# A spectral gate on one core: a rewritten order list, with cosine and sine parts of ten even and five odd row slots split between ScalarE and VectorE

## The chip, the cores and the metric

The kernel runs on one core of one Trainium2 chip. The metric is device time in microseconds for one execution. Before the change the median of three runs is 117.61 us (117.53 to 118.46).

A core has five instruction streams that run side by side and wait for one another through semaphores. TensorE (PE) multiplies matrices into PSUM. VectorE (DVE) and ScalarE (ACT) copy, cast and combine; both read PSUM. GpSimd (POOL) does element-wise work on SBUF. SyncE (SP) issues almost all DMAs here. Each stream executes its instructions in the order in which they stand, so an instruction that waits holds back everything behind it on its own engine.

## The reference

```python
def _A_ref(x, w_r, w_i):
    X = rfft2(x.astype(float32), axes=(-2, -1))
    X = X * (w_r + 1j * w_i)
    return irfft2(X, s=(S, D), axes=(-2, -1)).astype(bfloat16)
...
x = A_x
g = sigmoid((x * gate_w).sum(-1, keepdims=True))
return g * _A_ref(x, A_w_r, A_w_i) + (1 - g) * _B_ref(x, B_w_r, B_w_i)
```

x is 2048 x 1024 in bfloat16. Both filters act on the same x, so the forward transform is made once, multiplied by two sets of weights, and the two inverse transforms are mixed with the gate g, one number for each row.

## The kernel before, in words

All transforms are matrix multiplications. The 2048 rows are 16 groups s1 of 128; the 1024 columns are folded four ways, so that the even and the odd column frequencies (parity 0 and 1) are two separate problems of half the size.

The program is written out by hand. A string `ORDER` holds some 590 tokens, and a loop at the end calls one small function for each token. Nothing is rescheduled: the order of the tokens is the order on each engine's stream and on SP's DMA stream. A token names the step, its indices, the PSUM banks (0 to 7) that it uses, and for copies the engine (A for ScalarE, D for VectorE, P for GpSimd). The steps, with the lines that the profile shows for them:

- `x`, `c`, `W`: loads of x, of constants and of the 16 weight tiles (L252 to L264, L276), all on SP but for two small ones, the constant F1 and the gate column gws, which ScalarE issues. Each of the eight DMA slots of a queue is reused by the eighth DMA after it, which waits for it. `tab` (L298, L299) makes ScalarE load its function table.
- First stage. `F1:s1:e/o` (L334) multiplies row group s1 for one parity into half a bank for each of two halves; the two halves have to be added and subtracted into `y`. Either `FC` copies one half to a scratch tile (L204 on ScalarE, L206 on VectorE) and `FD` folds on VectorE (L382, two instructions), or `FX` copies both and `FP` folds on GpSimd (L382 on POOL, two instructions). The scratch tiles are eight slots in `wx`, used in turn (`tmp`). `gc` prepares gate coefficients on GpSimd and needs gws.
- Middle stage, for n = 0 to 15 (0 to 7 even, 8 to 15 odd). `F2` (L450) and its copies `T`, `F3` (L480) and its copy `X`, `P` (L494, VectorE: two products of 128x2048 elements with the weights), `J` (L537), whose result two copies `R` bring to SBUF tiles `rl` (five in use at once), and two `H` (L549) that store them, 256 KB each, to a scratch area in DRAM. `NA` and `N` patch one column. `GH` to `GW` make the gate and multiply it into the matrices EA and EB.
- The turn through DRAM. `L:par:v` (L554) reads 512 KB of the scratch back in another layout; each needs all H of its parity.
- Last stage, for eight row slots v and two s. `V:par:v:s` (L565) and its copy `VC`, then `U` (L581) or `C` (L590). `U` gives the row transform for both halves of the columns; `C`, half the matmul columns, gives its cosine and sine parts, whose sum and difference are the two halves. For the even parity the result is kept in `EV`: `EX` copies both parts to scratch and `EQ` (L615) adds and subtracts them, or `E` copies. For the odd parity `OR` (L635, VectorE) adds or subtracts EV and the PSUM bank into the output tile, `OC` and `OP` (L631) do so through a copy and GpSimd, `QD` and `QP` (L642, L647) for parts. `S` (L652) stores the slot.

What orders the stages: `y` of all groups of one parity before its `F2`; H of a parity before its L; L:0 before `V:0`; L:1 before `V:1`.

Of the kernel before, what the change touches and what calls it, by code (L numbers as in the profile page):

```python
# [24 lines left out]
warm:8 c:A:F1 c:A:gws tab:A x:S:0:1 x:S:1:1 x:S:2:2 x:S:4:2 x:S:6:2 x:S:8:2 x:S:10:2 x:S:12:2 x:S:14:2 c:S:FD:0:1  # L25
F1:1:o:0 F1:1:e:1 FX:1:o:D F1:0:o:2 FC:1:e:D F1:0:e:3 FP:1:o FD:1:e F1:3:o:0 F1:2:e:4 FC:0:e:D F1:3:e:1 gc:P FD:0:e
F1:2:o:5 FC:3:e:A FC:2:e:D F1:4:e:3 FD:3:e FX:2:o:A F1:5:o:6 FX:0:o:A FD:2:e F1:5:e:5 FC:4:e:A FP:0:o FX:3:o:A FD:4:e
F1:6:e:1 FC:5:e:A F1:4:o:2 FD:5:e FC:6:e:A F1:7:e:0 FP:2:o c:S:WF:0:4 FD:6:e F1:6:o:3 W:S:0 FC:7:e:A F1:9:e:7 FD:7:e
FX:6:o:A F1:8:e:1 FP:3:o FC:9:e:D c:S:WJ:0:4 F1:11:e:3 FD:9:e F1:10:e:0 c:S:w0 FC:11:e:A F1:7:o:4 c:S:PM FC:8:e:A
FP:6:o FD:11:e FX:5:o:A c:S:EZ F1:13:e:5 FC:10:e:A FD:8:e W:S:1 F1:12:e:6 FP:5:o FD:10:e c:S:WF:4:16 FC:12:e:A  # L30
F1:14:e:1 FC:13:e:A FD:12:e FX:4:o:A F1:15:e:3 W:S:2 F1:15:o:0 FD:13:e FP:4:o FC:15:e:A F1:11:o:2 FC:14:e:A FD:15:e
FC:15:o:A F1:8:o:6 c:S:WJ:4:16 F1:14:o:5 FD:14:e FC:8:o:A F1:10:o:3 neg:A:0:4 FD:15:o FC:14:o:A F1:12:o:7 FX:7:o:A
# [680 lines left out]
```

## Time and profile before

| | us |
|---|---|
| median of three runs | 117.61 |
| span of the profiled execution | 115.6 |
| PE busy in the span | 103.6 |
| VectorE busy | 97.0 |
| ScalarE busy | 84.4 |
| GpSimd busy | 46.2 |
| first F1 matmul | 4.87 |
| first product (P) starts | 24.53 |
| first even read-back (L:0:0) issued | 62.28 |
| first odd read-back issued | 83.95 |
| first odd V matmul | 89.17 |

Groups of the page that the change touches (line, engine, operation, out<-in, count; busy and mean ns of one; idle time before them and what ended it):

```profile
L615 POOL TENSOR_TENSOR re<-wx 128x256 f32<-128x256 f32 x28 | 19.6, 730 | 55.3 <-DMA re<-sc 53.1
L204 ACT CAST rl<-ps 128x1024 bf16<-128x1024 f32 x29 | 29.6, 1142 | 0.7 <-ACT wx L204 0.7
L494 DVE TENSOR_TENSOR p<-X,ro 128x2048 bf16<-128x2048 bf16 x16 | 19.1, 1215 | 0.0
L382 DVE TENSOR_TENSOR y<-ps,wx 128x256 bf16<-128x256 f32 x48 | 16.4, 412 | 0.1
L635 DVE TENSOR_TENSOR ot<-re,ps 128x512 bf16<-128x512 f32 x22 | 13.8, 681 | 0.4
```

Two instructions that follow each other on an engine overlap a little, so in a run of equal ones the distance from start to start is less than the mean time of one. The distance is what counts when work is summed.

### The profile page before, as it was taken

The numbers are of one execution on the slowest core, as the hardware profiler recorded it, in microseconds if no ns is written. First come the engines' busy times: TensorE is split into PE (matmuls) and PEld (weight loads), VectorE is DVE, ScalarE is ACT, GpSimd is POOL, SyncE is SP. The second block draws the span as 40 slices with busy tenths as digits, with TensorE's granted clock in tenths as the row PEclk, the third lists the DMA queues.
The fourth block names the chain that finished last, engine by engine and source line by source line (L and its number), as shares of the span: only waits on it lengthen the run. The fifth ranks groups of instructions, "written<-read, shape, count | busy, mean of one in ns | idle before, by whom it ended". The sixth has DMA issues, their size and how long they took to land.

```text
span 115.6 us, 3953 instructions
## 1 busy us (share of the span) xinstructions
PE 103.6 (90%) x1619; PEld 71.3 (62%) x1619; DVE 97.0 (84%) x164; ACT 84.4 (73%) x138; POOL 46.2 (40%) x74
## 2 busy tenths in 40 slices
PE   5999999999999699898889899989979999999900
PEld 2499989875567256463445357459859765867400
DVE  0099999999999999999899999999157349999970
ACT  4009488999999999999999999977735844534300
POOL 1066995900000000000000000057986999999920
PEclk9999999999999999999999999999999999999995
DMA  3999999999579999669999999999999992482874
GB/s 90 348 326 401 403 374 367 363 397 408 210 222 324 371 394 373 169 263 397 350 293 354 348 306 401 254 357 382 352 353 411 403 418 98 198 346 119 327 279 181
DMA packets 17794, 36.79 MB, mean 318 GB/s; under 512 B 1904, under 2 KB 10736, under 8 KB 17776
## 3 DMA queue, kind: packets, MB, share of 16 engines
q1 hardware_dynamic: 17488, 36.44, 87.5%
q8 instruction: 12, 0.20, 0.6%
q10 hardware_dynamic: 288, 0.10, 0.4%
q14 instruction: 6, 0.05, 0.1%
HBM read 23.96 MB, written 12.58 MB: 316 GB/s over the span
## 4 chain that ended last, share of the span: by engine, by line
PE 39%; DVE 19%; DMA 16%; ACT 16%; issue 4%; SPq 1%; DVEq 1%; ACTq 0%
ACT rl L204 11%; PE ps L581 9%; PE ps L565 8%; DVE y L382 7%; PE ps L450 6%; PE ps L334 5%; DMA sc<-rl 5%; DMA re<-sc 4%; DMA ig<-cst_ig 4%; PE ps L537 3%; DMA re<-in_x_dram 3%; PE ps L480 3%; DVE p L494 3%; ACT X L204 3%; PE ps L590 3%
## 5 line engine op out<-in xcount | busy, mean ns | idle before, releaser
L615 POOL TENSOR_TENSOR re<-wx 128x256 f32<-128x256 f32 x28 | 19.6, 730 | 55.3 <-DMA re<-sc 53.1
L204 ACT CAST rl<-ps 128x1024 bf16<-128x1024 f32 x29 | 29.6, 1142 | 0.7 <-ACT wx L204 0.7
L204 ACT COPY wx<-ps 128x256 f32<-128x256 f32 (+1 forms) x39 | 17.2, 498 | 10.5 <-PE ps L334 8.2
L537 PE MATMUL ps<-p,wj 32*64 32x512 bf16 x512 | 20.5, 381 | 2.5 <-ACT rl L204 2.0
L204 ACT CAST V<-ps 128x512 bf16<-128x512 f32 x25 | 13.8, 601 | 11.3 <-PE ps L565 8.4
L494 DVE TENSOR_TENSOR p<-X,ro 128x2048 bf16<-128x2048 bf16 x16 | 19.1, 1215 | 0.0
L450 PE MATMUL ps<-fd,y 128*128 128x256 bf16 x128 | 16.5, 273 | 0.4 <-ACT rl L204 0.4
L382 DVE TENSOR_TENSOR y<-ps,wx 128x256 bf16<-128x256 f32 x48 | 16.4, 412 | 0.1
L334 PEld LDWEIGHTS <-re 128*128 128x128 bf16 x256 | 15.2, 100 | 1.6 <-DMA re<-in_x_dram 1.0
L334 PE MATMUL ps<-f,re 128*128 128x128 bf16 x256 | 15.8, 224 | 0.3
L204 ACT CAST T<-ps 128x512 bf16<-128x512 f32 x26 | 15.5, 693 | 0.0
L537 PEld LDWEIGHTS <-wj 32*64 32x64 bf16 x512 | 8.4, 103 | 10.6 <-issue 7.5
L382 POOL TENSOR_TENSOR y<-wx 128x256 bf16<-128x256 f32 x16 | 11.1, 734 | 8.2 <-DVE wx L206 5.9
L635 DVE TENSOR_TENSOR ot<-re,ps 128x512 bf16<-128x512 f32 x22 | 13.8, 681 | 0.4
L450 PEld LDWEIGHTS <-y 128*128 128x128 bf16 x128 | 11.5, 97 | 4.1 <-issue 2.6
L581 PE MATMUL ps<-ig,V 128*128 128x512 bf16 x56 | 13.4, 380 | 0.0
L204 ACT CAST X<-ps 128x1024 bf16<-128x1024 f32 x12 | 13.2, 1118 | 0.0
L206 DVE COPY wx<-ps 128x512 f32<-128x512 f32 (+1 forms) x10 | 5.8, 578 | 7.4 <-PE ps L334 4.8
L480 PE MATMUL ps<-T,wf 64*64 64x256 bf16 (+1 forms) x128 | 10.2, 332 | 1.1 <-DVE np L514 1.0
L590 PE MATMUL ps<-ig,V 128*128 128x256 bf16 x72 | 9.7, 273 | 0.0
L494 DVE TENSOR_TENSOR p<-X,wx 128x2048 bf16<-128x2048 bf16 x8 | 9.4, 1217 | 0.0
L494 DVE TENSOR_TENSOR p<-X,y 128x2048 bf16<-128x2048 bf16 x8 | 9.3, 1215 | 0.0
(60 smaller groups left out, 138.4 us busy)
## 6 DMA issues: line engine op xcount, KB each, us to landing
sc<-rl SPq DMA_DIRECT2D x32, 256.0 KB, 4.7
ro<-in_we_dram SPq DMA_DIRECT2D x8, 512.0 KB, 8.3
re<-sc SPq DMA_DIRECT2D x8, 512.0 KB, 6.1
ro<-sc SPq DMA_DIRECT2D x8, 512.0 KB, 7.7
re<-in_x_dram SPq DMA_DIRECT2D x7, 512.0 KB, 8.0
out_dram<-ot SPq DMA_DIRECT2D x7, 512.0 KB, 2.6
wx<-in_wo_dram SPq DMA_DIRECT2D x4, 512.0 KB, 6.6
y<-in_wo_dram SPq DMA_DIRECT2D x4, 512.0 KB, 5.0
```

Source lines behind the costliest of these rows:

```text
L204: nc.scalar.copy(out=out, in_=in_)
L334: nc.tensor.matmul(o, lhsT=lh, rhs=rh, start=(h == 0), stop=(h == 1))
L382: Q[e].tensor_tensor(yo[:, v, k:k + n, s1, :], a.rearrange("p (k c) -> p k c", c=4), b.rearrange("p (k c) -> p k c", c=4), op)
L450: nc.tensor.matmul(ps[:, v * 256:v * 256 + 256], lhsT=y[:, v, par, b, 2 * t:2 * t + 2, :, :].rearrange("p j s c -> p (j s c)"), rhs=C["FD" ...
L480: nc.tensor.matmul(view(ps[ho, tt * 512:(tt + 1) * 512], dst), lhsT=lh, rhs=view(T[hp(jh), tt, :], src), start=(w == 0), stop=(w == 1))
L494: nc.vector.tensor_tensor(p[:, r], xb, w, ALU.mult)
L537: nc.tensor.matmul(o, lhsT=lh, rhs=src[r, ri, wi, tt], start=(q == 0), stop=(q == 3))
L565: nc.tensor.matmul(ps[:, ch * 128:ch * 128 + 128], lhsT=RR[par][:, v, ch // 2, s, c0 + 256 * ab:c0 + 256 * ab + 128], rhs=Ew[:, s1, :], st ...
L581: nc.tensor.matmul(ps, lhsT=Vs[par, v][:, s, ch, :], rhs=rh, start=(ch == 0), stop=(ch == 3))
L590: nc.tensor.matmul(ps[:, o:o + 256], lhsT=Vs[par, v][:, s, ch, :], rhs=g[:, o:o + 256], start=(ch % 2 == 0), stop=(ch % 2 == 1))
L615: Q[e].tensor_tensor(EV[:, v, s, 256 * h:256 * h + 256], t[:, 0], t[:, 1], (ALU.add, ALU.subtract)[h])
L635: nc.vector.tensor_tensor(otile(v)[:, s, h, :], EV[:, v, s], PS["O", 1, v, s], (ALU.add, ALU.subtract)[h])
```

## The change

`ORDER` is replaced as a whole; three functions change and two are new. The arithmetic of the result is the same.

```diff
 ORDER = """
-warm:8 c:A:F1 c:A:gws tab:A x:S:0:1 x:S:1:1 x:S:2:2 x:S:4:2 x:S:6:2 x:S:8:2 x:S:10:2 x:S:12:2 x:S:14:2 c:S:FD:0:1
...
-F3:13:6 R:10:0:A P:12:0 X:13:A H:10:0 J:11:0:4 L:0:4 P:12:1 R:10:1:A F3:14:6 R:11:0:A X:14:D F2:15:0:2 F2:15:1:3
-T:15:0:A P:13:0 T:15:1:A J:12:0:6 R:11:1:A V:0:0:1:2 P:13:1 R:12:0:A F3:15:4 V:0:0:0:3 R:12:1:D X:15:A H:12:0
-V:0:1:0:0 H:10:1 V:0:1:1:1 L:0:5 VC:0:1:0:A P:14:0 H:11:0 J:13:4:6 VC:0:0:0:A VC:0:1:1:A P:14:1 VC:0:0:1:A R:13:0:A
-P:15:0 J:14:0:2 R:13:1:A H:13:0 H:11:1 C:0:0:1:4 P:15:1 H:12:1 C:0:0:0:5 EX:0:0:D R:14:0:D R:14:1:A EX:0:1:A H:14:1
-J:15:6:2 H:13:1 EQ:0:1:0:P V:0:2:0:4 EQ:0:0:0:P C:0:1:1:5 R:15:0:D R:15:1:A H:14:0 C:0:1:0:0 EQ:0:0:1:P H:15:1
-V:0:2:1:1 VC:0:2:0:A GW:D:8 V:0:3:1:2 H:15:0 EX:1:1:A L:0:6 V:0:3:0:3 VC:0:2:1:A EX:1:0:D L:0:7 EQ:1:1:0:P C:0:2:0:4
-VC:0:3:0:D VC:0:3:1:A C:0:2:1:1 EQ:1:0:0:P V:0:4:1:0 EX:2:1:D EQ:0:1:1:P V:0:4:0:5 C:0:3:0:2 EQ:2:1:0:P VC:0:4:0:A
...
-L:1:7 C:0:6:1:2 EQ:2:1:1:P EX:6:1:A EQ:5:1:0:P VC:0:7:0:A VC:0:7:1:D E:3:1:D C:0:7:1:3 V:1:0:0:1 V:1:0:1:4 EQ:4:1:0:P
...
-S:S:3 OR:6:1:0 S:S:6
...
+warm:8 tab:A c:A:F1 x:S:0:1 F1:0:e:7 F1:0:o:1 x:S:8:2 c:S:WF:0:4 F1:9:e:5 F1:8:e:2 FC:0:e:D FC:0:o:A FD:0:e x:S:1:1 FD:0:o
+c:A:gws x:S:14:2 F1:8:o:6 F1:9:o:3 F1:1:e:1 F1:1:o:7 neg:P:0:4 FC:9:e:A gc:P FX:8:e:A FD:9:e F1:14:o:0 x:S:10:2 FC:8:o:D
+FX:1:e:A FC:1:o:A F1:15:o:2 FP:8:e F1:14:e:5 x:S:2:2 F1:15:e:1 FC:9:o:D x:S:4:2 FD:8:o FC:14:o:A F1:10:o:6 FD:9:o FX:15:o:A
...
+F1:3:o:6 FD:6:e FD:6:o FC:5:o:A FC:3:o:A F1:12:o:0 F2:1:0:5 FX:12:o:A FD:5:o F2:1:1:1 c:S:EZ T:1:0:A F2:0:1:3 T:1:1:A
+F1:2:o:4 F2:0:0:0 T:0:1:A FD:13:o FD:3:o F3:1:1 FC:2:o:D T:0:0:A F2:2:0:7 F3:0:5 F2:4:0:3 X:1:A c:S:PM c:S:WJ:0:4 W:S:2
+F2:4:1:0 FD:2:o X:0:A T:2:0:D FP:4:o FG:7:o:2 pw:P W:S:5 W:S:4 P:1:0 T:4:0:A FP:12:o P:1:1 Y:1:1 F2:2:1:6 W:S:0 T:4:1:A
+F3:4:4 NA:1:D FY:7:o:A T:2:1:A N:1:D W:S:8 P:0:0 c:S:FD:1:2 F2:3:0:7 P:0:1 F2:5:1:2 X:4:A F2:3:1:3 F3:2:0 T:3:0:A Y:4:7
...
+R:8:1:A F2:12:0:5 F2:11:0:2 T:11:0:D J:7:0:3 T:12:0:A R:7:0:A R:7:1:A P:10:0 P:10:1 F3:12:6 H:5:0 W:S:13 F3:11:0 X:11:A H:8:1
+F2:13:0:5 H:7:0 H:7:1 H:8:0 F2:14:1:2 J:10:3:0 GW:D:4:4 P:11:0 X:12:A T:13:0:A F2:13:1:5 L:0:3 P:11:1 R:10:0:A J:9:3:6
+GW:D:12:4 R:10:1:A T:13:1:A F2:14:0:5 R:9:1:A F3:13:0 R:9:0:D L:0:1 L:0:4 T:14:1:A T:14:0:D X:13:A L:0:2 L:0:0 J:11:3:6 L:0:6
+V:0:3:0:1 R:11:0:A R:11:1:A P:12:0 VC:0:3:0:A V:0:3:1:5 F2:15:1:4 F2:15:0:0 P:12:1 T:15:1:A L:0:7 VC:0:3:1:D J:12:2:6
+T:15:0:A H:11:1 H:11:0 F3:14:4 R:12:0:A X:14:A P:13:0 U:0:3:0:0 P:13:1 E:3:0:A V:0:0:0:3 H:10:1 H:12:0 J:13:1:4 H:9:1
+R:12:1:D VC:0:0:0:A P:14:0 P:14:1 V:0:0:1:7 R:13:0:A V:0:2:0:6 VC:0:0:1:A H:9:0 U:0:3:1:0 R:13:1:A H:13:1 F3:15:2 VC:0:2:0:D
+E:3:1:D V:0:2:1:1 X:15:A VC:0:2:1:D J:14:6:4 C:0:2:0:1 V:0:7:0:0 R:14:0:A C:0:0:1:3 C:0:0:0:7 V:0:1:0:2 P:15:0 EX:2:0:D
+R:14:1:A P:15:1 VC:0:7:0:A V:0:7:1:4 EX:0:1:A VC:0:7:1:A J:15:5:0 H:12:1 H:13:0 GW:D:8:4 L:0:5 C:0:2:1:3 VC:0:1:0:A EX:0:0:D
+R:15:0:A H:14:0 EX:2:1:A H:14:1 C:0:7:0:2 V:0:1:1:4 C:0:7:1:7 C:0:1:0:6 EQ:2:0:1:D EQ:2:0:0:P EQ:0:0:0:P EQ:0:1:0:P H:10:0
+EQ:2:1:0:P EQ:0:0:1:P ES:7:0:A R:15:1:D ES:7:1:A V:0:6:1:1 V:0:6:0:3 VC:0:1:1:A V:0:5:0:0 ES:1:0:A EF:7:0 VC:0:6:1:A H:15:0
+C:0:1:1:5 H:15:1 V:0:4:0:2 EF:1:0 VC:0:6:0:A V:0:5:1:6 EQ:0:1:1:P VC:0:5:1:A EF:7:1 ES:1:1:D C:0:6:0:1 VC:0:5:0:D L:1:1 L:1:3
+L:1:6 C:0:6:1:4 VC:0:4:0:A V:0:4:1:3 C:0:5:0:6 ES:6:0:A ES:5:0:A EQ:2:1:1:D EF:1:1 C:0:4:0:7 C:0:5:1:2 V:1:1:0:0 EF:6:0
...
+OF:1:1 OP:1:1:1 U:1:3:1:2 OS:3:0:A OP:1:1:0 VC:1:6:1:A L:1:5 V:1:4:0:5 OR:1:0:1 OF:3:0 OR:1:0:0 VC:1:6:0:A OP:3:0:1 C:1:6:1:1
...
+S:S:6:0 OR:0:0:1 OR:0:0:0 VC:1:5:0:A U:1:7:0:3 V:1:5:1:5 OP:0:1:1 OR:7:0:1 S:S:4 U:1:5:0:7 VC:1:5:1:A OR:7:0:0 S:S:2 OR:5:0:0
+OR:5:0:1 S:S:0:0 U:1:5:1:0 S:S:0:1 OR:5:1:1 S:S:7 S:S:5:0 OR:5:1:0 S:S:5:1
...
     def even_sin(v, s, e):
         v, s = int(v), int(s)
-        if ("E", v) not in TM:
-            TM["E", v] = tmp()
-        cp(e, TM["E", v][:, s], PS["O", 0, v, s][:, 256:512])
+        TM["E", v, s] = tmp()
+        cp(e, TM["E", v, s][:, 0], PS["O", 0, v, s][:, 256:512])
...
     def even_sum(v, s):
         v, s = int(v), int(s)
         for h, op in enumerate((ALU.add, ALU.subtract)):
-            nc.vector.tensor_tensor(EV[:, v, s, 256 * h:256 * h + 256], PS["O", 0, v, s][:, 0:256], TM["E", v][:, s], op)
+            nc.vector.tensor_tensor(EV[:, v, s, 256 * h:256 * h + 256], PS["O", 0, v, s][:, 0:256], TM["E", v, s][:, 0], op)
...
+    def odd_sin(v, s, e):
+        v, s = int(v), int(s)
+        TM["OS", v, s] = tmp()
+        cp(e, TM["OS", v, s][:, 0], PS["O", 1, v, s][:, 256:512])
+
+    def odd_fold(v, s):
+        v, s = int(v), int(s)
+        t = TM["O", v, s] = tmp()
+        for h, op in enumerate((ALU.add, ALU.subtract)):
+            nc.vector.tensor_tensor(t[:, h], PS["O", 1, v, s][:, 0:256], TM["OS", v, s][:, 0], op)
```

`ES`, `EF`, `OS`, `OF` are the tokens of these four functions; `FG` and `FY`, which stood unused in the kernel before, fold one odd group in the matmul itself (twice the columns of an F1) and copy the result straight to `y`. The tokens of both lists, counted by step and engine, where they differ:

| | before | after |
|---|---|---|
| first stage: FC on ScalarE, FX on ScalarE, FX on VectorE | 20, 7, 1 | 18, 9, 0 |
| first stage: FD on VectorE, FP on GpSimd | 24, 8 | 22, 9 |
| one odd group by FG and FY | 0 | 1 |
| T, X, R on ScalarE | 26, 12, 29 | 27, 14, 27 |
| T, X, R on VectorE | 6, 4, 3 | 5, 2, 5 |
| VC on ScalarE, on VectorE | 25, 7 | 28, 4 |
| even: EX, and EQ on GpSimd, EQ on VectorE | 14, 28, 0 | 4, 6, 2 |
| even: ES (ScalarE 7, VectorE 3), EF (VectorE) | 0, 0 | 10, 10 |
| odd: OC, OP, QD, QP | 3, 6, 4, 4 | 0, 10, 0, 0 |
| odd: OS (ScalarE), OF (VectorE) | 0, 0 | 5, 5 |
| odd: OR | 22 | 22 |
| U, C | 14, 18 | 13, 19 |
| stores S | 9 | 12 |

Row groups, units n and row slots v come in another sequence throughout: the first groups are 0, 9, 8, 1 and the x loads follow them; the middle stage runs n = 1, 0, 2 to 6, 8, 7, 10, 9, 11 to 15; the even slots come as 3, 0, 2, 7, 1, 6, 5, 4. Of the eight even read-backs, seven stand together between the stores of n = 8 and n = 11, and `L:0:5` stands after the stores of n = 13. In the list before, four stand together, a fifth and a sixth follow among the stores, and `L:0:6` and `L:0:7` stand after the store of n = 15. In ScalarE's stream the table load now comes ahead of the DMA for F1, and the DMA for gws comes behind the first copy.

## The prediction

> **What bounds the kernel now.** I read the page's busy rows by slices first, then the work of each engine in stretches, then the chain of waits, then single engines in order of time.
>
> ```profile
> PE   5999999999999699898889899989979999999900
> DVE  0099999999999999999899999999157349999970
> ACT  4009488999999999999999999977735844534300
> DMA  3999999999579999669999999999999992482874
> ```
>
> The third row is ScalarE. In the middle (slices of 2.89 us) ScalarE, VectorE and the DMA engines are full together, PE almost; after slice 27 VectorE and ScalarE fall to a half and PE stays full; from slice 33 VectorE is full again.
>
> ```profile
> 24.50:76.00 51.50, 47.44 (x943) 27.87 (x946) 50.52 (x68) 51.50 (x70) 0.00 (x0) 1.00 0.93 322
> ```
>
> This stretch runs from the first product to the last J (columns PE, weight load, VectorE, ScalarE, GpSimd with counts, clock, DMA share, GB/s). ScalarE idles 0, VectorE 1.0: whatever is added to either lengthens it.
>
> ```profile
> 79.96 0.39 SPq L549
> 80.35 0.05 issue
> 80.40 5.18 DMA re<-sc
> 85.58 0.05 issue
> 85.62 0.62 PE ps L565 x8
> ...
> 110.85 1.20 DVE ot L635 x2
> ```
>
> In the chain of waits the middle hands over to the read-back through DRAM, and the chain ends on VectorE's last output rows.
>
> ```profile
> L554 SPq DMA_DIRECT2D ro<-sc x3: 320/424/426, 84.0 to 84.8; - x3
> ...
> DMA to landing us min/median/max: 4.8/5.7/6.5
> ```
>
> The first odd read-back, issued at 83.95, lands 4.8 us later at 88.75; the first odd V runs at 89.17. So the odd half too starts on a DMA, with 0.4 us to spare.
>
> ```profile
> 94.94 5.24 DVE L635 TENSOR_TENSOR ot<-re,ps 128x512 bf16<-128x512 f32 x8
> 100.10 2.47 DVE L642 TENSOR_TENSOR pq<-re,ps 128x512 f32<-128x512 f32 x4
> 102.49 0.68 DVE L206 CAST V<-ps 128x512 bf16<-128x512 f32 x1
> 103.12 8.93 DVE L635 TENSOR_TENSOR ot<-re,ps 128x512 bf16<-128x512 f32 x14
> ```
>
> From 94.94 to 112.05 VectorE has no gap: the odd half takes 22.9 us from its first V to the last row, and 3.55 more to the end of the span (last store issued 112.1, landing 2.6, then 0.9). The profiled span is 115.6; the median 117.61 lies 2.0 above it, and I add that 2.0 at the end. I follow one time through the change, T0, the first odd V, because two things that are otherwise separate meet there.
>
> **The start: about 1.1 us lost.** ScalarE's stream now has the table load ahead of the DMA for F1.
>
> ```profile
> 0.71 0.38 ACTq L264 DMA_DIRECT2D f<-cst_f  x1
> 1.12 0.48 ACTq L259 DMA_DIRECT2D gws<-in_gw_dram  x1
> 1.64 1.28 ACT L299 ACT_TABLE_LOAD   x1 [1.64 <-PEq L693]
> 2.93 0.21 ACT L299 ACTIVATE junk<-junk 128x8 f32<-128x8 f32 x1
> ```
>
> If the load starts at 0.71, F1 is issued at 0.71+1.28+0.21 = 2.2 and lands 3.2 later (its own row) at 5.4; PE started at 4.87. Loss 0.5. gws now stands behind the first copy, at about 6.8, and lands 3.9 later at 10.7; GpSimd's coefficients (1.1, from 8.39 to 9.50 before) end at 11.8, and only then do its folds begin, which before ran from 6.72 and without a break from 10.47. Seven of them belong to even groups: 7 x 2 x 0.69 (8.30 for 12) = 9.7, so 21.5, while PE gets through its 30 F1 at 5.4 + 14.75 (4.87 to 19.62) = 20.2. F2 would start 0.5 (PE) to 1.9 (GpSimd) late; some of it is caught up before the first product, since two of F2's copies follow anyway. I take 1.1 for the first product (25.6 instead of 24.53); bounds 0.3 and 2.
>
> [...]
>
> **The middle: 2.9 us more on VectorE.** Between the first and the last product VectorE loses two T (0.60 each, start to start) and two X (1.14) and gains three R (1.14), three VC, an E and an EX (0.60 each): -1.2 -2.3 +3.4 +3.0 = +2.9. ScalarE, from the copy X:1 to the release of the last J, has 13 X for 11, 23 T for 22, 26 R for 28, FY, an E, and no 0.75 us negation: at 0.905 (X, R) and 0.48 (T, FY, E) that is +0.7, under VectorE's. The last product ended at 75.6; now 75.6 + 1.1 + 2.9 = 79.6.
>
> To this comes a wait. `L:0:3` needs the store of n = 7, which stands one unit later: ScalarE has 33.2 us of work from X:1 to that copy instead of 31.6, so it ends about 59.0; two issues of 0.4 and 4 us landing (3.5 to 4.7 in that stretch) put the first read-back at 63.8 instead of 62.28. The list has it earlier, the clock does not; only L:0:5 to L:0:7 gain. The seven stand in one queue. With 4 us for the first (5.0 was the least, behind more stores) and 1.4 for each 512 KB (1.26 odd, 1.5 even), the fifth, L:0:0, lands at 73.4. PE reaches `V:0:0:0` at about 71 to 72.5, and J:13 stands behind it on PE, R:13 on ScalarE, P:15 on VectorE behind VC:0:2:0. Bounds 0 (PE no earlier than the landing) and 2.2; I take 0.7, as VectorE is behind PE there. P:15:1 ends at 80.3.
>
> **The turn.** Behind P:15:1 VectorE has a gate step (0.79), EX (0.60), EQ (0.35) and R:15:1 (1.14): 83.2. Before, the last R ended at 78.56. H:15:1: 0.4 issue and 3.5 landing (rows: 2.3 least, 4.0 in this place): 87.1. L:1:1: 4.8 before, behind two even loads that are now ahead of H:15; I take 4.0: T0 = 91.1, 1.9 later than 89.2. Check by bytes: the DMA engines were full (shares 1.02, 1.04) from 62.28 to 88.75, 26.5 us, with the same stores and loads; counted from 63.8 the same work ends at 90.3, 0.8 before the sum above; the two ways agree to within the wait that I added.
>
> [...]
>
> GpSimd sheds 22 of 28 EQ (16 us). They were off the chain except as its neighbour, so I credit nothing. VectorE's ten EF (2 x 0.335) and three ES (0.35) come to 7.7 us, between 83.2 and T0+1.5; PE waits for read-back there, which covers them. If the turn were short, they would be late next.
>
> **The odd half: 1.7 us won.** VectorE needs 5 OF (0.67) and 22 OR (0.622), 17.0, as against 16.8 for 22 OR, 4 QD and a VC. But it begins sooner. Before, its first row stood behind VC:1:2:1, 5.6 us after T0. Now PE does three V (0.445), C (0.43), U (0.86), C (0.43) by T0+3.1, OS takes 0.3, and OF:1:1 starts at T0+3.5. Walking both streams, VectorE waits for PE about 0.7 in all and ends at T0+21.2 (before T0+22.9); PE has 19.2 and is no longer behind. GpSimd's ten OP at 1.27 end near T0+17.4, ahead of their store. Then the last store is half a slot, 2.0 landing instead of 2.6: 2.95 for 3.55. Sum: 91.1 + 21.2 + 2.95 = 115.25, 0.35 below the span. Forecast 117.3.
>
> **Rivals.** *The queue stays full and T0 does not move.* Without the idle third of 30 to 35 us (DMA share 0.58) and with short landings, T0 is 89.4 and the time 89.4 + 24.15 + 2.0 = 115.6. For it: H and L at their least (2.3 and 3.0). Against: R:15:1 must still come by 84.
>
> *Slower: the block of seven.* J:13 behind L:0:0, and R:14 behind H:11:0, whose slot it reuses and which now queues behind all seven. At 5.0 and 1.5 us L:0:7 lands at 77.8 and H:11:0 at 79.3; R:14 could run at 76. Through R:14, J:15, R:15 this adds 2.4: T0 93.5, time 119.7. It decides once L:0:0 lands more than 2 us after PE stands at V:0:0:0. For it: DMA shares over 1 and 8.8 us as the longest even landing. Against: VectorE is late there too.
>
> [...]
>
> **How the numbers follow.** A measurement of this kernel can tell 1% from no change: 116.4 and 118.8. Forecast 0.38, own range 116.1 to 118.5 from the landing bounds: 0.06 of it counts as faster, 0.04 as slower. Full queue 0.28 (114.2 to 116.2), all faster. Block of seven 0.29 (118.8 to 121), all slower. Drain 0.05, 0.02 slower. Faster 0.34, same 0.31, slower 0.35. Leaving a tenth at each end: 114.8 to 120.0.
>
> **What would show it.** PE's first F1 at 5.4 or later; GpSimd's first fold near 12; first product near 25.6, last ending near 80; first even read-back issued at 63 to 64, not earlier; PE or ScalarE idle before V:0:0:0 on `re<-sc`; L:1:1 landing near 91; from the first odd V to the last OR about 21 us. The forecast is wrong if the last product ends before 77, if T0 is under 89, or if VectorE is full through the odd half with more than 22 us.

## The result, and the profile after

The changed kernel takes 121.58 us (median of 4 runs, 120.34 to 122.84). The kernel before takes 117.63 us on the same chip. The ratio is 1.0346, with a 95% interval of 1.0233 to 1.0458: slower by 3.5%. The forecast was 117.3 us, and the result lies above the upper end of its range. The profiled execution took 121.54 us, and its span is 119.8 us. Here and below a median is over all executions of a kernel, while a ratio and its interval leave out those that took over 1.5% more than the fastest of the same kernel, so a ratio is not the quotient of two medians.

First the busy rows of the page of the changed kernel, in slices of 3.0 us, now with GpSimd's row and the granted clock.

```profile
PE   6988659999999999979896996998995699999930
DVE  0197199999999999999999999699798258899990
ACT  4046278999999999999999998887957147645500
POOL 0030999990000000000000000005920006998700
PEclk9999999999999999999999999999999679999996
DMA  3999999869998598899994999999925999129993
```

There are two new places to look at. In slices 5 and 6 (12 to 18 us) TensorE falls to six and five tenths, and VectorE almost stops in slice 5, while GpSimd is full from slice 5 to slice 9. In slices 31 and 32 (90 to 96 us) TensorE falls to five and six tenths, and in slices 32 and 33 the clock to six and seven.

The stretch from the first product to the end of the last one has this row (columns: TensorE, weight load, VectorE, ScalarE, GpSimd with counts, clock, DMA share, GB/s). Before, the same stretch was 51.17 us long (24.53 to 75.70), and VectorE was busy for 50.19 of it.

```profile
26.48:81.80 55.32, 51.53 (x995) 31.02 (x992) 53.64 (x72) 53.47 (x72) 1.53 (x2) 1.00 0.93 324
```

VectorE has 3.45 us more to do, and idles 0.7 us more. The chain of waits then goes from a copy R of the last slice through its stores and the odd read-back to the first odd V, and ends on VectorE, as before:

```profile
83.94 1.03 ACT rl L200
84.98 0.36 SPq L545
85.44 4.42 DMA sc<-rl
90.06 3.79 DMA ro<-sc
93.89 1.89 PE ps L561 x16
...
116.05 0.60 DVE ot L630
```

The first odd read-back is issued at 90.06 (before: 83.95) and the first odd V runs at 93.89 (before: 89.17). The 16 matmuls of the first two odd V take 1.89 us here. VectorE's odd half, as its own rows in order of time show it, waits 3.06 us for TensorE at its beginning, and is full at its end:

```profile
96.67 0.42 DVE L202 COPY wx<-ps 128x256 f32<-128x256 f32 x1 [3.06 <-PE ps L586]
...
110.37 6.28 DVE L630 TENSOR_TENSOR ot<-re,ps 128x512 bf16<-128x512 f32 x10
```

This table follows the same marks through the profiled executions (us from the start of the span). T0 is the first odd V, as in the prediction. The first two columns after the prediction are the changed kernel and the same with gws loaded first; the last two are experiments that are told below.

| mark | before | predicted | after | gws first | combined | last slice rewritten |
|---|---|---|---|---|---|---|
| first product | 24.53 | 25.6 | 26.48 | 24.72 | 24.35 | 24.64 |
| last product ends | 75.70 | 80.3 | 81.80 | 80.32 | 80.00 | 76.63 |
| last R ends | 78.56 | 83.2 | 85.2 | 83.7 | 83.4 | 81.2 |
| T0 | 89.17 | 91.1 | 93.89 | 91.88 | 91.84 | 90.34 |
| T0 to the last OR | 22.88 | 21.2 | 22.76 | 21.17 | 21.17 | 21.18 |
| span | 115.6 | 115.25 | 119.8 | 116.2 | 116.1 | 114.6 |
| median of runs | 117.63 | 117.3 | 121.58 | 119.31 | 117.85 | 116.35 |

### The profile page after: what moved, and what is told of

Its sections match the earlier page's. It is cut to its first block, busy times and chain, and to the rows that moved or that the text cites. A ratio compares the mean times of both kernels' runs of the same rounds, so it can differ in the third digit from the quotient of the medians.

```text
span 119.8 us, 3963 instructions
## 1 busy us (share of the span) xinstructions
PE 103.5 (86%) x1619; PEld 71.1 (59%) x1619; DVE 100.2 (84%) x182; ACT 87.8 (73%) x145; POOL 34.2 (29%) x55
## 5 line engine op out<-in xcount | busy, mean ns | idle before, releaser
L200 ACT CAST rl<-ps 128x1024 bf16<-128x1024 f32 x27 | 27.0, 1034 | 1.3 <-PE ps L533 1.3
L200 ACT CAST V<-ps 128x512 bf16<-128x512 f32 x28 | 16.1, 594 | 12.2 <-PE ps L561 8.8
L610 POOL TENSOR_TENSOR re<-wx 128x256 f32<-128x256 f32 x6 | 5.3, 898 | 55.4 <-DVE wx L202 53.8
L490 DVE TENSOR_TENSOR p<-X,ro 128x2048 bf16<-128x2048 bf16 x16 | 19.4, 1240 | 0.0
L533 PE MATMUL ps<-p,wj 32*64 32x512 bf16 x512 | 18.4, 380 | 0.5 <-ACT rl L200 0.3
L626 POOL TENSOR_TENSOR ot<-re,wx 128x512 bf16<-128x512 f32 x10 | 12.4, 1278 | 13.0 <-DVE wx L641 12.9
L378 POOL TENSOR_TENSOR y<-wx 128x256 bf16<-128x256 f32 x18 | 12.4, 722 | 0.0
L561 PEld LDWEIGHTS <-ro 128*128 128x128 bf16 x128 | 9.2, 107 | 4.7 <-DMA ro<-sc 2.8
L561 PE MATMUL ps<-ea,ro 128*128 128x128 bf16 x64 | 9.6, 236 | 2.6 <-DMA ro<-sc 2.6
L586 PE MATMUL ps<-ig,V 128*128 128x256 bf16 x76 | 11.1, 281 | 0.7 <-ACT V L200 0.7
L476 PE MATMUL ps<-T,wf 64*64 64x512 bf16 (+1 forms) x128 | 10.4, 333 | 1.3 <-ACT T L200 0.7
```

The lines of the kernel that those rows point to most:

```text
L200: nc.scalar.copy(out=out, in_=in_)
L378: Q[e].tensor_tensor(yo[:, v, k:k + n, s1, :], a.rearrange("p (k c) -> p k c", c=4), b.rearrange("p (k c) -> p k c", c=4), op)
L476: nc.tensor.matmul(view(ps[ho, tt * 512:(tt + 1) * 512], dst), lhsT=lh, rhs=view(T[hp(jh), tt, :], src), start=(w == 0), stop=(w == 1))
L490: nc.vector.tensor_tensor(p[:, r], xb, w, ALU.mult)
L533: nc.tensor.matmul(o, lhsT=lh, rhs=src[r, ri, wi, tt], start=(q == 0), stop=(q == 3))
L561: nc.tensor.matmul(ps[:, ch * 128:ch * 128 + 128], lhsT=RR[par][:, v, ch // 2, s, c0 + 256 * ab:c0 + 256 * ab + 128], rhs=Ew[:, s1, :], st ...
```

## The experiments

The order list is the only thing that the edits below touch. All ratios are to the kernel before on the same chip.

### The start: where gws stands

In the changed kernel two rows of GpSimd, four of ScalarE and its queue and one of TensorE, each in order of time, show the start:

```profile
11.74 0.24 POOL L286 TENSOR_SCALAR gh<-gws 128x8 f32<-128x8 bf16 x1 [4.26 <-DMA gws<-in_gw_dram]
...
12.80 4.83 POOL L378 TENSOR_TENSOR y<-wx 128x256 bf16<-128x256 f32 x7
```

```profile
0.71 1.28 ACT L295 ACT_TABLE_LOAD   x1 [0.71 <-PEq L699]
0.86 0.36 ACTq L260 DMA_DIRECT2D f<-cst_f  x1
...
5.90 0.36 ACTq L255 DMA_DIRECT2D gws<-in_gw_dram  x1
...
14.24 0.65 ACT L200 COPY wx<-ps 128x256 f32<-128x256 f32 x2 [2.82 <-POOL y L378]
```

```profile
16.24 1.95 PE L330 MATMUL ps<-f,re 128*128 128x128 bf16 x32 [2.24 <-ACT wx L200]
```

The load of gws is issued at 5.90 and lands 5.8 us later. GpSimd waits 4.26 us for it, and its first fold runs at 12.80. ScalarE's copies go to a ring of eight scratch tiles that the folds empty, so ScalarE then waits 2.82 us for GpSimd, and TensorE 2.24 us for ScalarE. The load of F1, on the other hand, is issued at 0.86, in the middle of the table load. The first experiment puts gws back ahead of the table load.

```diff
-warm:8 tab:A c:A:F1 x:S:0:1
+warm:8 c:A:F1 c:A:gws tab:A x:S:0:1
...
-FD:0:o c:A:gws x:S:14:2
+FD:0:o x:S:14:2
```

> The changed kernel with the head of ScalarE's stream as before: F1, gws, then the table load. Theory (the start): in the changed kernel gws is issued at 5.90, GpSimd's first fold starts at 12.80, ScalarE and PE stand still on GpSimd's scratch slots (2.8 and 2.2 us), and the first product starts at 26.48 instead of 24.53. With gws early the first fold starts before 9.5, PE has no wait on ScalarE near 14 to 16, the first product starts at 24.4 to 25.2, and the time falls by 1.2 to 2.0 us. Rival: the loss at the start is taken up later, because the read-back through DRAM sets the odd half anyway; then the first product comes earlier but the time falls by less than 0.5.

Measured: 119.31 us, ratio 1.0047 (0.9985 to 1.0108). The first fold runs at 8.44, the first product at 24.72, and T0 comes at 91.88. Moving one 2 KB load takes back most of the 3.5%: three points by this ratio, two by that of the same kernel run once more below (1.0147). This edit also changes when the table is loaded, so a second one leaves both loads where the change has them, and only takes GpSimd's coefficients out of the way of its folds.

```diff
-neg:P:0:4 FC:9:e:A gc:P FX:8:e:A
+neg:P:0:4 FC:9:e:A FX:8:e:A
...
-F1:4:e:4 FP:3:e FC:11:o:A
+F1:4:e:4 FP:3:e gc:P FC:11:o:A
```

> The changed kernel as it is, with its late load of gws, and one edit: GpSimd's gate coefficients stand behind its fourth pair of folds instead of ahead of the first. Theory (the start is lost because every fold of GpSimd waits for gws through the coefficients): the first fold runs near 8 instead of 12.8, the coefficients near 13.5, TensorE's idle time between 10 and 16 falls under 1 us, the first product starts at 24 to 25 instead of 26.5, and the time is that of the kernel with gws loaded first, 118.5 to 120. Rival (the new order of F1 or the table load ahead of F1 costs too): the first product stays after 25.5 and the time at 120.5 or more.

Measured: 118.61 us, ratio 1.0102 (1.0044 to 1.016). The first fold runs at 8.55, and the first product at 24.62. Two different edits that share only the removal of GpSimd's wait bring the first product to the same place. The new order of F1 and the early table load cost nothing that shows. The converse, the late gws (and with it the early table load) in the list of the kernel before:

```diff
-warm:8 c:A:F1 c:A:gws tab:A x:S:0:1
+warm:8 tab:A c:A:F1 x:S:0:1
...
-F1:3:e:1 gc:P FD:0:e
+F1:3:e:1 FD:0:e
...
-FC:3:e:A FC:2:e:D
+FC:3:e:A c:A:gws gc:P FC:2:e:D
```

> The kernel before, with only the start of its list changed in the way the change has it: the table load first, the load of gws behind ScalarE's first copy, and GpSimd's coefficients straight behind that. Theory (the late gws, through GpSimd's folds, is what the start loses): the load is issued near 6.5, lands near 11.5, GpSimd's second fold begins near 12.7 instead of 9.5, the first product starts 1 to 2 us later than 24.53, and the whole comes out 1 to 2 us later, 118.6 to 119.7. Rival (the new order of F1, not gws, is what costs): the first product stays within 0.4 us of 24.53 and the time within 0.5 us of the kernel before, 117.3 to 118.1.

Measured: 124.94 us, ratio 1.0636 (1.0552 to 1.072). The direction is the theory's, but the 7.5 us are nearly four times the upper end of what was expected. The reason is in GpSimd's rows and in two windows (columns as above):

```profile
15.72 0.24 POOL L287 TENSOR_SCALAR gh<-gws 128x8 f32<-128x8 bf16 x1 [7.55 <-DMA gws<-in_gw_dram]
```

```profile
14.96:21.58 6.62, 0.01 (x2) 0.00 (x0) 1.97 (x6) 1.28 (x4) 5.70 (x13) 0.84 0.86 290
21.58:26.00 4.42, 4.42 (x42) 4.42 (x42) 3.87 (x12) 2.38 (x7) 3.49 (x6) 0.50 1.01 384
```

There ScalarE's first copy waits longer, so gws is issued at 8.49. TensorE then idles 6.62 us, and afterwards works at a clock of 0.50 until 26. The first product comes 8.1 us late, at 32.66.

### The block of seven read-backs

The prediction's slower rival was that V:0:0:0 waits for the fifth of seven read-backs in one queue. This edit puts the seven in the order of their use.

```diff
-L:0:3
+L:0:3
...
-L:0:1 L:0:4
+L:0:0 L:0:2
...
-L:0:2 L:0:0
+L:0:7 L:0:1
...
-L:0:7
+L:0:5
...
-L:0:5
+L:0:4
```

> The changed kernel with the eight even read-backs at the same places but in the order in which V uses them (3 0 2 7 1 6 5 4 instead of 3 1 4 2 0 6 7 5). Theory (the block of seven): V:0:0:0 waits until 73.5 for the fifth read-back and holds J:13 and the last products; as the second it lands near 69.5, the wait of PE (0.95) and the one of VectorE (1.1) go, and the last product ends 0.8 to 1.5 us earlier, the time with it. Rival: the last products are bound by VectorE's work alone, and the time falls by less than 0.4.

Measured: 121.63 us, ratio 1.0329 (1.0176 to 1.0483). The runs cannot tell this from the changed kernel, but the interval is wide enough to hide 1 us. In the profiled execution TensorE's wait for even read-backs falls from 1.1 to 0.5 us, and T0 comes 66.2 us after the first product instead of 67.4. So the block may cost up to about 1 us, which is not shown by the times; it is not what makes the loss of 4 us.

### Even mixing and odd parts, each undone

Does VectorE's share of the even mixing (ES and EF) cost time? This gives it back to GpSimd, in all ten rows.

```diff
-ES:7:0:A
+EX:7:0:A
...
-EF:7:0
+EQ:7:0:0:P EQ:7:0:1:P
...
```

> The changed kernel with its ten split even row slots back on EX and EQ (ScalarE or VectorE copies both parts, GpSimd adds and subtracts) instead of ES and EF. This gives VectorE 5.5 us less and GpSimd 14.6 us more between 85 and 100. Theory: EF lies in the time in which PE waits for the odd read-back, so it costs nothing and taking it away wins nothing (within 0.5 us, or slower where GpSimd's EQ and OP run into each other: GpSimd would have 17 us of work from 84 and 12.4 of OP behind it, ending near 115). Rival: the mixing on VectorE is itself what lengthens the end, and the time falls by 1 us or more.

Measured: 125.23 us, ratio 1.0512 (1.0364 to 1.066). No gain, so ES and EF are not where the time goes. Nor are the 3.6 us above the changed kernel all the price of the mixing: the span of the profiled execution is 4.7 us longer, and 3.7 of that lie ahead of the first product, at 30.19, after a lowered clock at the start (0.50 from 16.4 to 23.3), where the list is unchanged. From there to T0 it took 67.2 us, as in the changed kernel (67.4). Another 1.0 us lies behind the last OR, and could be the edit's. Next, with gws first, the five split odd rows become whole rows again.

```diff
-C:1:1:1:5
+U:1:1:1:5
...
-OS:1:1:A
+OC:1:1:A
...
-OF:1:1 OP:1:1:1
+OP:1:1:1
...
```

> The changed kernel with gws loaded first, and the five split odd rows taken back to whole rows: TensorE does eight matmuls of 512 columns again in place of the parts, ScalarE copies 512 columns, and the five folds on VectorE are gone. Theory (the split shortens the odd half, where TensorE was the later engine): from the first odd V to the last output row 22.5 to 24 us, against some 21 with the split, and the time 120.0 to 121.5 against 119.3. Rival (VectorE sets the odd half, its five folds cost 3.4 us): the stretch gets shorter, 20 us or less, and the time falls to 118.5 or under.

Measured: 120.93 us, ratio 1.0304 (1.0219 to 1.039). The stretch from T0 to the last OR is, without the split and with it:

```profile
92.04:115.32 23.28, 21.36 (x192) 13.64 (x196) 15.87 (x28) 11.62 (x21) 12.46 (x10) 1.00 0.78 308
```

```profile
91.88:113.05 21.17, 19.46 (x196) 13.66 (x196) 18.95 (x38) 10.51 (x21) 12.44 (x10) 1.00 0.85 337
```

The split takes 1.9 us off TensorE and puts 3.1 on VectorE, which had room. The odd half is 2.1 us shorter by it. This is the part of the change that works. OF:1:1 starts 3.7 us after T0 with the split.

### The clock at the first odd V

In the changed kernel the stretch from T0 took 22.76 us and not 21.17, with the same matmuls. Windows around T0:

```profile
91.33:93.89 2.56, 0.00 (x1) 0.00 (x1) 2.29 (x7) 0.61 (x3) 0.00 (x0) 0.98 0.89 341
93.89:97.20 3.31, 3.31 (x28) 3.06 (x29) 0.53 (x2) 1.17 (x2) 0.00 (x0) 0.50 1.02 402
97.20:100.00 2.80, 2.80 (x33) 2.24 (x32) 2.06 (x7) 1.75 (x4) 0.00 (x0) 1.00 1.03 408
```

TensorE idles 2.56 us before the read-back lands, and the next 3.3 us run at a clock of 0.50. That is about 1.6 us of work lost. The first attempt at it, on the changed kernel:

```diff
-C:0:5:1:2 V:1:1:0:0
+C:0:5:1:2 warm:10:0 V:1:1:0:0
```

> The changed kernel with ten matmuls of zero use (128x128 by 128x512, into the bank that the next V overwrites) ahead of the first odd V, where PE stands idle for 2.56 us. Theory (the clock): the granted clock falls to 0.50 from 93.9 to 97.2 because PE stood idle; kept busy it stays at 1.00, the first 16 odd V matmuls take 0.9 instead of 1.7 us, and the time falls by 1.3 to 1.8 us. Rival: the clock falls for another reason (power, or the stage itself), it falls here too, and the time stays or grows by up to 0.3.

Measured: 122.66 us, ratio 1.03 (1.0177 to 1.0424), no gain. At T0 it did what was expected: the clock stays at 1.00, and T0 to the last OR is 21.17. But in this profiled execution the clock fell earlier, from 16.4 to 19.8 us, after the idle time at the start, and the first product came at 28.21. So the run could not settle what the fall at T0 is worth. A pair with gws first, where the start is quiet, can: the same kernel with five dummy matmuls (warm:5:0 at the same place) and without.

> The changed kernel with gws loaded first and, as the only other edit, five dummy matmuls ahead of the first odd V. Theory (with gws first, the clock still falls at the first odd V in most executions, only not in the profiled one, and costs 1.6 us there): the first odd V runs no later than 92.5, the median is 0.8 to 1.6 us below that of the kernel without dummies on the same chip, 117.6 to 118.5, and the single times lie closer together. Rival (the 119.3 of the kernel with gws first against its profiled 117.9 has another cause): both medians within 0.4 us.

> The changed kernel with gws loaded first once more, as the pair of the kernel with five dummies. Theory: median near 119.3, with single times in two groups, near 117.7 where the clock stays at 1.00 at the first odd V and near 119.4 where it falls to 0.50; a profiled execution of the second group shows T0 to the last output row as 22.8 us instead of 21.2. Rival: one group, and no lowered clock in the profiled execution whatever its time.

Measured: 118.36 us with dummies (ratio 1.0101, 1.0052 to 1.0151) and 119.31 without (1.0147, 1.0089 to 1.0205), so 0.95 us, inside what the theory expected. The profiled execution without dummies took 119.29 us and shows the fall (the one with dummies took 116.87). First its windows, then the one window at the same place with dummies:

```profile
89.33:91.61 2.28, 0.00 (x1) 0.01 (x1) 2.28 (x7) 0.61 (x3) 0.00 (x0) 1.00 0.87 332
91.61:95.40 3.79, 3.79 (x30) 3.14 (x31) 1.29 (x5) 1.55 (x3) 0.00 (x0) 0.55 1.03 413
```

```profile
90.83:94.20 3.37, 3.37 (x42) 2.80 (x43) 1.89 (x6) 1.75 (x4) 0.00 (x0) 1.00 1.03 413
```

T0 to the last OR is 22.82 us in the one and 21.17 in the other. The two intervals overlap, so the size of the gain is less sure than its mechanism. Nor are the two groups of times clear that the expectation named. Of the 16 executions of the kernel without dummies on two chips, the nine with a mean granted clock of 0.978 to 0.982 have a median of 119.42 us, and the seven with 0.991 to 0.998 one of 118.18, but three of these seven took 119.22 to 120.0 us. So the fall is a part of what lies between the 117.93 us of the first profiled execution with gws first, which has no fall, and its median of 119.31; what else spreads the times stays open.

### The middle: the last slice's place

Once gws is first, the products up to P:14:1 run nearly as early as before: P:14:1 starts at 73.0 us there, and at 72.2 in the kernel before. What comes late is P:15:0 and P:15:1. VectorE's rows in order of time, first of the kernel before and then of the changed kernel:

```profile
71.08 4.62 DVE L494 TENSOR_TENSOR p<-X,y 128x2048 bf16<-128x2048 bf16 x4
```

```profile
73.58 2.35 DVE L490 TENSOR_TENSOR p<-X,y 128x2048 bf16<-128x2048 bf16 x2
77.05 0.69 DVE L202 CAST V<-ps 128x512 bf16<-128x512 f32 x1 [1.11 <-PE ps L577]
77.66 0.68 DVE L202 COPY re<-ps 128x512 f32<-128x512 f32 x1
78.26 0.68 DVE L202 CAST V<-ps 128x512 bf16<-128x512 f32 x1
78.86 1.22 DVE L490 TENSOR_TENSOR p<-X,y 128x2048 bf16<-128x2048 bf16 x1
79.98 0.69 DVE L202 COPY wx<-ps 128x512 f32<-128x512 f32 x1
80.58 1.22 DVE L490 TENSOR_TENSOR p<-X,y 128x2048 bf16<-128x2048 bf16 x1
```

Before, the last four products stand together. Now a wait of 1.11 us and four copies of 0.6 us of the even inverse stand between them. If VectorE's load is what counts, giving three of these copies to ScalarE brings them back.

```diff
-VC:0:2:0:D
-E:3:1:D
+VC:0:2:0:A
+E:3:1:A
...
-VC:0:2:1:D
+VC:0:2:1:A
```

> The changed kernel with gws loaded first, and three copies that stand among the last products (the two V copies of row 2 and one even row's copy) given from VectorE to ScalarE, which idled 1.5 us between 70 and 80. Theory (VectorE carries the middle to its end, so 0.6 us per copy comes back): last product ends near 78.8 instead of 80.3, the odd read-back is issued near 87 instead of 88.2, and the time is 1.0 to 1.8 us under the 119.3 of the kernel with gws alone: 117.5 to 118.3. Rival (the read-backs and ScalarE's R copies set the end of the middle): the last product ends at 80 or later and the time stays within 0.5 us of 119.3.

Measured: 119.22 us, ratio 1.0174 (1.0088 to 1.0259); no gain over gws alone. The last product ends at 81.16, later than the 80.32 without the edit. In VectorE's rows of this kernel a wait has taken the place of the copies:

```profile
71.86 2.35 DVE L490 TENSOR_TENSOR p<-X,y 128x2048 bf16<-128x2048 bf16 x2
78.12 1.23 DVE L490 TENSOR_TENSOR p<-X,y 128x2048 bf16<-128x2048 bf16 x1 [3.91 <-ACT X L200]
```

P:15:0 now waits 3.91 us for X:15, because F3:15 on TensorE and X:15 on ScalarE also stand behind even inverse work in the list. The three edits so far and five dummies together:

> The changed kernel with four edits: gws loaded first, the seven even read-backs in the order of their use, three copies given from VectorE to ScalarE, and five dummy matmuls ahead of the first odd V. If the single effects add up (119.3 for gws alone, 0.4 off for the order of the read-backs, 1.0 to 1.8 off for the copies, 0 to 0.5 off for a clock that is not lowered): 116.8 to 118.0, with VectorE's wait in the middle under 0.5 us. Rival (the turn through DRAM takes up what the middle gives): the time stays at 118.8 or more, and the odd read-back lands no earlier than 91.5.

Measured: 117.85 us, ratio 1.0017 (0.997 to 1.0065). The whole loss is gone, yet the last product still ends at 80.00, with 2.83 us of waiting for X:15. What it gained over gws alone is then, as far as the pair above tells, mostly the clock at T0: the idle time there is 0.96 us, and the clock stays at 1.00.

Then F3:15 and X:15 were taken forward, in three kernels that did not tell what they were meant to:

```diff
-J:13:1:4 H:9:1 R:12:1:D
+J:13:1:4 F3:15:6 H:9:1 R:12:1:D
...
-V:0:0:1:7 R:13:0:A V:0:2:0:6
+V:0:0:1:0 R:13:0:A X:15:A V:0:2:0:3
```

> The kernel with the four edits together, and besides TensorE's F3 of the last slice and ScalarE's copy X:15 taken ahead of the even inverse work that stands before them (F3:15 goes to banks 6 and 7 behind J:13; two V take banks 0 and 3). Theory (VectorE's idle 2.8 us before P:15:0 is the place in which the list puts F3:15 and X:15, so the end of the middle is set by order, not by VectorE's load): P:15:0 starts near 75 instead of 76.97, the last product ends near 78, the odd read-back is issued near 86.5, the first odd V runs near 90.3, the time is 1 to 2 us under the 117.85 of the four edits, 115.9 to 116.9. Rival (the even read-back sets PE's pace, so what is taken ahead is lost behind it): the odd read-back is issued at 87.5 or later and the time stays at 117.3 or more.

> As the kernel with the last slice early, and VectorE's gate step GW for rows 8 to 11 taken from behind the last product to ahead of P:15:0. Theory: its 0.95 + 0.42 us leave the path between the last product and R:15:1, and GpSimd is idle at its new place, so its first half takes 0.41 us; the last R ends up to 1 us earlier and the time falls by 0.3 to 1.0 us, to 115.2 to 116.5. Rival (J:15 on TensorE, not VectorE, is what R:15:1 waits for): the last R ends within 0.3 us of where it did and the time does not move.

> As the kernel with the gate step early, without the five dummy matmuls ahead of the first odd V, so that TensorE idles some 2 us there. Theory (an idle TensorE of 2 us or more lowers the granted clock for some 3 us in part of the runs): the median is 0.3 to 1.0 us above that of its pair, or the single times spread wider, up to 1.6 us above. Rival (2 us are too short, the clock falls only after longer idle time): both within 0.3 us.

In these three F3:15 goes to two banks of PSUM ahead of R:12:1, which still has to copy slice 12 from them; R:12:1 copies other data, and stands behind X:15. So these kernels no longer store the right slice 12, and VectorE waits some 2.4 us at R:12:1, ahead of the last products, for nothing. Measured: 119.0 us (ratio 1.0107, 1.0064 to 1.0149), 119.73 (1.016, 1.0109 to 1.021) and 119.41 (1.0135, 1.0091 to 1.0178). They say nothing of the order of the last slice, and for the gate step and the dummies, which lie behind that wait, they are inconclusive.

The stretch was then written anew with F3:15 behind R:12:1. These are its main tokens:

```diff
-V:0:0:1:7 R:13:0:A V:0:2:0:6 VC:0:0:1:A
...
-U:0:3:1:0 R:13:1:A
...
-F3:15:2 VC:0:2:0:D
-E:3:1:D V:0:2:1:1 X:15:A VC:0:2:1:D J:14:6:4 C:0:2:0:1 V:0:7:0:0 R:14:0:A C:0:0:1:3 C:0:0:0:7 V:0:1:0:2 P:15:0 EX:2:0:D
-R:14:1:A P:15:1
...
-J:15:5:0
+F3:15:6 P:14:0 P:14:1 U:0:3:1:0 R:13:0:A X:15:A V:0:0:1:1 V:0:2:0:2 R:13:1:A
...
+VC:0:0:1:A P:15:0 VC:0:2:0:A J:14:6:4 E:3:1:A V:0:2:1:3 P:15:1 R:14:0:A R:14:1:D C:0:2:0:0 VC:0:2:1:A J:15:1:6
+H:14:0 H:14:1 GW:D:8:4 V:0:7:0:3 C:0:0:1:4 C:0:0:0:5 R:15:0:A R:15:1:D H:15:0 H:15:1 V:0:1:0:2
```

> The changed kernel as it is, late gws included, with the last slice's stretch of the list rewritten and nothing else. Theory (start and last slice are two separate losses that add up): first product still near 26.5, last R near 83 instead of 85.2, first odd V near 91.5 instead of 93.9, time 118.5 to 120 instead of 121.58. Rival (the odd half starts on the read-back whatever the last R does): the first odd V stays at 93 or later and the time at 121 or more.

> The kernel with gws first, even read-backs in order of use and three copies on ScalarE, with the last slice's stretch of the list rewritten: F3:15 and X:15 behind R:12:1 and ahead of the even inverse work, J:14 and J:15 ahead of most of it, R:14:1 and the gate step on VectorE behind P:15:1, R:15 and its stores behind J:15. It computes the reference. Theory (products 1 to 30 run as early as in the kernel before, and the loss of the middle is only what the list puts before P:15:0, P:15:1 and R:15): P:15:0 starts near 75 instead of 77, the last product ends at 77 to 78, the last R at 80 to 81.5 instead of 83.4, the first odd V runs at 89 to 90.5, the time is 115.3 to 117. Rival (VectorE's and ScalarE's whole load of the middle sets it, or TensorE's even inverse work only moves behind): the last R ends at 82.5 or later, or the first odd V stays at 91.3 or later, and the time at 117.5 or more.

> As the kernel with the last slice rewritten, with five dummy matmuls ahead of the first odd V. Theory (TensorE then has no idle time of 2 us in which the clock could be lowered): in the profiled run the clock stays at 1.00 at the first odd V; the median is 0 to 0.8 us below its pair where the pair still idles 1.5 us or more, and up to 1 us above it where the dummies (1.2 us) only stand in the way of a read-back that has landed. Rival (the dummies do nothing to the time): both within 0.3 us.

On the changed kernel alone: 121.79 us, ratio 1.0366 (1.0307 to 1.0426), no gain. From the first product (28.45) to the end of the last one (81.91) it takes 53.46 us instead of 55.32, so the place in the list does account for 1.9 us of the middle; a wait for X:15 is left. But T0 comes 67.4 us after the first product, in both kernels. In this one, TensorE has even inverse work left before T0, and waits in it for a read-back that now stands behind the last stores (VectorE's row of the last two products, then TensorE's):

```profile
79.55 2.36 DVE L490 TENSOR_TENSOR p<-X,y 128x2048 bf16<-128x2048 bf16 x2 [1.66 <-ACT X L200]
```

```profile
91.40 0.23 PE L561 MATMUL ps<-ea,re 128*128 128x128 bf16 x1 [1.03 <-DMA re<-sc]
```

Here the rival was right: what is taken ahead moves other work behind. (In this profiled execution the clock also fell at the start, to 0.50 from 16.8 to 20.2, and the first product came at 28.45.)

With gws first, the read-backs in order of use and the three copies on ScalarE, the same stretch gives 116.35 us, ratio 0.9864 (0.9813 to 0.9916): faster than both kernels, by 1.4% against the kernel before. The last products stand together again (VectorE's rows), and the clock does not fall anywhere (the page's row):

```profile
71.74 2.35 DVE L490 TENSOR_TENSOR p<-X,y 128x2048 bf16<-128x2048 bf16 x2
74.27 2.36 DVE L490 TENSOR_TENSOR p<-X,y 128x2048 bf16<-128x2048 bf16 x2 [0.19 <-ACT X L200]
```

```profile
PEclk9999999999999999999999999999999999999999
```

T0 comes 65.7 us after the first product, 1.8 earlier than in the combined kernel, and TensorE has no idle time before it. So five dummies, which the combined kernel has too, can only stand in the way: with them T0 comes 67.3 us after the first product, much as in the combined kernel, and the time is 117.40 us (0.9962, 0.9918 to 1.0006), T0 is 91.19 instead of 90.34, and the 1.05 us is what the expectation gave as their upper price. So most of what the rewritten stretch gains is lost again when five dummies stand ahead of T0.

## Why the prediction was wrong, step by step

The forecast's sum for the span was 115.25, and the span is 119.8. The 4.55 us between them, by the marks of the table: first product 0.9, first to last product 0.6, last product to last R 0.5, last R to T0 0.8, T0 to the last OR 1.6, end 0.2. (The 2.0 from span to median came out as 1.8.) Two terms failed most. The odd half was put at 21.2 with nothing for the clock, and took 22.76; the late start was put at 1.1, and took 1.95.

**The start, "about 1.1 us lost": wrong in one part and too small in the other.** The part on F1 was wrong: the table load does not hold the DMA issue behind it (0.86, inside 0.71 to 1.99), and TensorE's first F1 ran at 4.55, earlier than before, not at 5.4. No run shows the drain that the chances put at 0.05: the next ACTIVATE starts at 2.01, 0.02 us after the load ends. The part on gws named the right path, from gws through the coefficients to the folds, and its mark came out (first fold expected near 12, measured 12.80), but by some luck: the load was issued at 5.90 and not 6.8, and took 5.8 us to land and not 3.9. But the sum compared when GpSimd ends its folds with when TensorE ends its F1. It left out the ring of eight scratch tiles in between, through which a late GpSimd stops ScalarE and TensorE in the middle (2.82 and 2.24 us). It cost 1.95, about the upper bound of 2, and the two experiments that remove GpSimd's wait bring all but 0.1 to 0.2 of it back.

**The middle, "2.9 us more on VectorE" and 0.7 of waiting: about the right size, but not a sum that one can take back by load.** Measured are 3.45 and 0.7. Some 0.35 of it is the first product pair, 2.70 us instead of 2.35 beside a GpSimd fold. The reading that VectorE carries the middle fell: with three copies taken off VectorE, a wait for X:15 came in their place. Nor does the extra work lengthen the middle evenly. With gws first, P:15:1 starts 4.6 us later than before (79.1 and 74.5), and all of that but 0.8 us arises behind P:14:1, where the list has put the even inverse ahead of the last slice on three engines at once.

**The turn: the last R half a microsecond and the landings 0.8 us off.** Between the last product and R:15:1 the gate step took 1.33 us, start to start, where 0.79 was counted. In the changed kernel it meets GpSimd's first EQ (VectorE's rows, then GpSimd's):

```profile
81.72 0.95 DVE L435 TENSOR_TENSOR ea<-ea,e 128x512 bf16<-128x512 bf16 x1
82.71 0.43 DVE L436 TENSOR_TENSOR eb<-e,ea 128x512 bf16<-128x512 bf16 x1
```

```profile
80.75 1.64 POOL L610 TENSOR_TENSOR re<-wx 128x256 f32<-128x256 f32 x1 [53.79 <-DVE wx L202]
```

EQ's mean was 0.73 before, and the gate step's first half took 0.41; here they take 1.64 and 0.95. (EQ had begun beside P:15:1, which runs from 80.58 to 81.80.) With the gate step where GpSimd is idle, as with the last slice rewritten and gws first (it starts at 78.44 there, and GpSimd has no work from 70 to 80), its first half took 0.41. Then H:15:1 landed in 4.42 instead of 3.5, and L:1:1 in 3.79 instead of 4.0.

**The odd half, "1.7 us won": right in its mechanism, and given back in the changed kernel.** OF:1:1 was put 3.5 us behind T0 and starts 3.7 behind it with gws first (the first row before stood 5.8 behind, not 5.6). T0 to the last OR was put at 21.2. It is 21.16 to 21.21 in every profiled execution with the split in which the clock stays at 1.00 at T0, and undoing the split costs 2.1 us of it. In the changed kernel the halved clock takes 1.6 of it away. No step of the prediction asked what TensorE's idle time before T0 does to the clock: it used that idle time only as cover for EF and ES, and in that it was right (giving them back to GpSimd won nothing).

**The rivals.** The block of seven was the slower rival. The result lies on its side, but its mechanism is a small part at most. V:0:0:0 did wait, until 73.53, where the prediction had L:0:0 land at 73.4; TensorE lost 0.95 us there and VectorE 1.11, and the sum had taken 0.7. With the read-backs in order of use T0 comes 1.2 us sooner after the first product in one profiled execution, and the times show no gain. A full queue that leaves T0 in place, at 89.4, did not come about: in the changed kernel H:15:1 took 4.42 to land and L:1:1 3.79, T0 was 93.89, and the earliest T0 of the table's kernels with the new list is 90.34. The case that happened, the start and the clock, was in none of them: the fault is less in the single bounds than in adding them as if a stall had no second price.

## What to carry to other kernels

When a small load moves behind other work, follow not only who reads it, but what stands behind that reader in its queue, and through which ring of buffers that queue feeds the others; here 2 KB cost some 2 us. A stall that empties TensorE for about 2 us may be charged twice, once as the wait and once as half-clock work behind it (2.56 and 1.6 us before and behind T0 here), so a gain in the half that follows should not be counted until the wait is gone. And where an order list interleaves two stages, look at the last piece of the first stage on every engine: taking its obstacles off one engine only makes the next engine's order the bound.

## What the runs showed of the hardware that was not expected

The granted clock fell to 0.50 after quite short idle times of TensorE, but the length of the idle time does not decide alone. It fell after 2.56 us before T0 in the changed kernel, 2.28 in the pair's kernel without dummies, 2.12 with the coefficients behind the folds, 2.06 with the read-backs in order of use, and, going by the four matmuls behind the wait, which took 1.75 us, after 1.92 in the middle of the kernel with the gate step early and no dummies. It stayed at 1.00 after 2.57 us at the start with the read-backs in order of use, 2.34 before T0 with the three copies on ScalarE, 2.04 in the first run with gws first, 1.98 with the odd split undone, 1.06 in the pair's kernel with dummies, and 1.92 in the middle of the kernel with the last slice early, where the same four matmuls took 1.02 us.

In the changed kernel the granted clock goes down at 93.81, up at 97.23 and down again at 117.71, behind the last output row: 3.42 and 20.48 us lie between, one and six times 3.41. In other profiled executions a low stretch lasted as long (16.4 to 19.8 with ten dummies, 16.8 to 20.2 with the last slice rewritten alone) or twice as long (16.4 to 23.3 with the even mixing given back, 19.4 to 26.2 in the kernel before with late gws). Counted back from 93.81 in stretches of 3.41 us, two stretches share the changed kernel's 2.24 us of waiting at the start, and one holds the 2.56 us before T0 (columns as above):

```profile
11.89:15.31 3.42, 1.96 (x32) 1.84 (x33) 0.67 (x2) 0.65 (x2) 3.26 (x9) 1.00 1.02 398
15.31:18.72 3.41, 2.48 (x45) 2.48 (x45) 3.15 (x11) 2.77 (x8) 3.41 (x6) 1.00 1.06 388
```

```profile
90.40:93.81 3.41, 0.93 (x9) 0.59 (x6) 3.08 (x9) 1.52 (x5) 0.00 (x0) 1.00 0.74 255
93.81:97.23 3.42, 3.34 (x28) 3.09 (x29) 0.56 (x2) 1.17 (x2) 0.00 (x0) 0.50 1.02 402
```

With 1.96 and 2.48 us of TensorE work in them the clock stayed at 1.00, and behind the stretch with 0.93 it was 0.50. So it is, from 5 us on, with all stretches at full clock of this profiled execution and of that of the kernel before (there counted back from 112.13, where its clock goes down): three have 0.64, 0.93 and 1.31 us of TensorE work, and the clock was 0.50 behind each; all others have 1.96 or more, and it was 0.50 behind none. These are two executions, the 0.64 and the 1.31 lie at their ends, and no run set this share on purpose. That the same wait is costly where one such stretch holds most of it, and free where two share it, is the author's reading of them, and was not shown by a run of its own.

At the start the clock could fall too: in three other profiled executions with the late gws (ten dummies; even mixing given back; last slice rewritten alone) TensorE waited 3.13 to 3.42 us instead of 2.24, the clock fell at 16.4 to 16.8 us, and the first product came at 28.21, 30.19 and 28.45 instead of 26.48.
